# Output projections of all query blocks placed behind the attention loop, with three quarters of the next sum over the sequence

## The chip, the core and the metric

The kernel runs on one core of one Trainium2 chip. The metric is the device time of one execution in microseconds (us). A core has engines that run side by side, each with its own instruction queue: PE (TensorE, matrix products into PSUM), DVE (VectorE), ACT (ScalarE), POOL (GpSimd), and SP, which here does nothing but issue DMA transfers. PEld is the loading of PE's stationary operand. An instruction waits in its queue for the semaphores of what it needs, and what stands behind it in the same queue waits with it.

## What is computed

Four layers on x of 2048 positions by 512 features in bf16: a spectral layer (A), an attention layer (B), and both once more, each with a layer norm in front and a residual sum behind.

```python
def _A_ref(x, w_r, w_i):
    X = jnp.fft.rfft2(x.astype(jnp.float32), axes=(-2, -1)) * (w_r + 1j * w_i)
    return jnp.fft.irfft2(X, s=(S, D), axes=(-2, -1)).astype(jnp.bfloat16)

def _B_ref(x, wq, wk, wv, wo):          # 32 heads of 16, one key and value head
    q = (x @ wq).reshape(B, S, H, Dh).transpose(0, 2, 1, 3)
    k, v = x @ wk, x @ wv
    p = _softmax(jnp.einsum("bhqd,bkd->bhqk", q, k) * (Dh ** -0.5))
    o = jnp.einsum("bhqk,bkd->bhqd", p, v)
    return o.transpose(0, 2, 1, 3).reshape(B, S, H * Dh) @ wo

x = x + _A_ref(_layernorm(x), A_w_r, A_w_i)
x = x + _B_ref(_layernorm(x), B_wq, B_wk, B_wv, B_wo)
x = x + _A_ref(_layernorm(x), A_w_r, A_w_i)
x = x + _B_ref(_layernorm(x), B_wq, B_wk, B_wv, B_wo)
```

## The kernel before

x stays in SBUF as x_sb, 16 tiles of 128 positions by 512 features, named by r and t (position = 512 r + 4 p + t, p being the partition); xn_sb holds the normalised tiles in the same arrangement.

**Spectral layer.** The transform over the sequence is a matrix product by tables, split by t. over_s(t) takes, for each of four feature blocks b, four matmuls of xn_sb against the table FT (L218) and lets ACT copy the sum from PSUM into G (L220). DVE then combines the four t (over_t_even, over_t_odd: L228 to L239) into X, and over_d multiplies X by the feature table (L272). The way back ends in back_s, which writes x_sb and normalises it for the attention. Three calls of over_s come before over_t_even, the fourth behind it. The table FT has 2 MB and is loaded by four DMAs from SP (L202) into a buffer that the attention's transposed input xT used before it.

**Attention loop.** 32 groups g of four heads: group g belongs to query block g // 8 (512 positions). For each group and 16 blocks of keys there are 64 score tiles of 128 by 512. ACT takes three of every four (exponential of three tiles at once, L647), and DVE the fourth, by an integer trick in two instructions (L671, L677). So one group is 16 steps of the loop, and a layer 514. Each step issues its scores on PE (L569), the exponential, DVE's two instructions, and the product with the values of the step LAG = 2 before (pv_step, L659). That product and a row of denominators add up in one PSUM bank (pool psp, one buffer) over the group.

At the end of a group DVE copies that bank to o (evict, L584). The denominators are row 16 of each 32 and must be inverted and spread over the partitions: o to DRAM (d), back as 128 by 16 (den), a reciprocal on DVE (L592), to DRAM again, and four broadcast loads to rb (L597). POOL multiplies o by rb in three pieces (L614), each paced by DVE's work. Groups of even number write straight into ot (bf16, four column blocks for a query block); odd ones write od, and four DMAs (L617) move it 16 partitions on. At the end of a group the same PSUM bank also serves the query projection for group g + 2 (L437, copied by L442).

**Output projection.** When a query block is complete, outproj(k) multiplies a tile of 128 positions by wo in four matmuls (L627); DVE adds the residual (L631) and the layer norm follows: statistics on DVE (L142, L144), the rest on POOL (L148 to L153). In the last layer a DMA stores the tile instead (L774, by SP and POOL in turn). For the first three query blocks these 12 calls stand inside the loop, one in each of four groups (out_at), with the same PSUM bank; in such a step pv_step is put off. The last four calls stand behind the loop, after the denominators of group 31.

**Order.** chain() ties the instructions of PE, ACT, DVE and POOL inside the attention layer to the order in which the program issues them; SP's transfers are not tied. Elsewhere a scheduler orders them. The PSUM of the attention layer is six banks for two score buffers of three (psc), one for DVE's score tile (psd), one for psp.

Of the kernel before, what the change touches and what calls it, by code (L numbers as in the profile page):

```python
# [139 lines left out]
def layernorm_tile_pool(nc, lnpool, tabs, x_ap, xn_ap):  # L140
    stats = lnpool.tile([P, 6], F32, tag="ln_stats", bufs=4)
    nc.vector.bn_stats(stats, x_ap)  # L142
    mv = lnpool.tile([P, 2], F32, tag="ln_mv", bufs=4)
    nc.vector.bn_aggr(mv, stats)  # L144

    def rest():
        rstd = lnpool.tile([P, 1], F32, tag="ln_rstd", bufs=4)
        nc.gpsimd.tensor_scalar(out=rstd, in0=mv[:, 1:2], scalar1=EPS, scalar2=1.0, op0=ALU.add, op1=ALU.mult)  # L148
        nc.gpsimd.tensor_tensor(out=rstd, in0=rstd, in1=tabs["mhalf"], op=ALU.pow)
        nb = lnpool.tile([P, 1], F32, tag="ln_nb", bufs=4)  # L150
        nc.gpsimd.tensor_scalar(out=nb, in0=mv[:, 0:1], scalar1=rstd, scalar2=-1.0, op0=ALU.mult, op1=ALU.mult)
        for a in (0, 256):
            nc.gpsimd.tensor_scalar(out=xn_ap[:, a:a + 256], in0=x_ap[:, a:a + 256], scalar1=rstd, scalar2=nb,  # L153
                                    op0=ALU.mult, op1=ALU.add)
    return rest


R_OUTER = [(k // 4, k % 4) for k in range(16)]
# [32 lines left out]
def spectral_layer(nc, tc, tabs, shared, lnpool, x_sb, xn_sb, WT, WX, aw, loads):  # L191
# [5 lines left out]
    with (tc.tile_pool(name="workA", bufs=1) as work,  # L197
          tc.tile_pool(name="psA", bufs=6, space=bass.MemoryType.PSUM) as psum,
          tc.tile_pool(name="psB", bufs=2, space=bass.MemoryType.PSUM) as psum_b):
        FT = shared.tile([P, T, R, 512], BF, tag="big", bufs=1)  # L200
        for t in range(T):
            nc.sync.dma_start(out=FT[:, t], in_=tabs["src"]["FT"][:, t])  # L202
# [6 lines left out]
        G = work.tile([P, 4, T, 514], BF, tag="big", bufs=2)  # L209
        X = work.tile([P, 4, 2, 2, 4, 128], BF, tag="big", bufs=2)  # L210
        g.memset(G[:, :, :, 256:257], 0.0)


        def over_s(t):
            for b in range(4):
                ps = psum.tile([P, 512], F32, tag="pa")
                for r in range(R):
                    nc.tensor.matmul(ps, lhsT=xn_sb[:, r, t, b * P:(b + 1) * P], rhs=FT[:, t, r, :],  # L218
                                     start=(r == 0), stop=(r == R - 1))
                nc.scalar.copy(out=G[:, b, t, :].rearrange("p (s j) -> p s j", j=257)[:, :, 0:256],  # L220
                               in_=ps.rearrange("p (s j) -> p s j", j=256))
# [132 lines left out]
        U = work.tile([P, T, 2, 2, 512], BF, tag="big", bufs=2)  # L354
# [32 lines left out]
        for t in range(3):  # L387
            over_s(t)
# [35 lines left out]
def attention_inputs(nc, tabs, shared, xn_sb, aw):  # L424

    wq_sb, wka, wv_sb, vaug = aw["wq"], aw["wk"], aw["wv"], aw["vaug"]
    xT = shared.tile([P, NC, R * T, P], BF, tag="big", bufs=1)
# [3 lines left out]
    xTq = xT.rearrange("d c t p -> d c (t p)")  # L431
    QT = {}

    def qproj(g, ps):
        qb, hg = divmod(g, HG)
        for c in range(NC):
            nc.tensor.matmul(ps, lhsT=wq_sb[:, c, hg, :], rhs=xTq[:, c, qb * 512:(qb + 1) * 512],  # L437
                             start=(c == 0), stop=(c == NC - 1))
# [7 lines left out]
    def block(t, psum):  # L446
        for half in range(2):
# [4 lines left out]
            k = 4 * t + 2 * half  # L452
            dst = xT[:, :, k:k + 2, :].rearrange("d c i p -> d i c p")
# [6 lines left out]
        for c in range(NC):  # L460
            nc.tensor.matmul(ps, lhsT=wka[:, c, :], rhs=xTq[:, c, ks], start=(c == 0), stop=(c == NC - 1))
# [4 lines left out]
        for i in range(4):  # L466
            for c in range(NC):
                nc.tensor.matmul(psv[:, i, :], lhsT=xT[:, c, 4 * t + i, :], rhs=wv_sb[:, c, :],
# [25 lines left out]
def attention_layer(nc, tc, tabs, x_sb, xn_sb, aw, prep, epilogue_cb, in_order):  # L494
    with ExitStack() as ctx:
# [49 lines left out]
        for n0 in range(s0[NG]):  # L545
# [7 lines left out]
            if n in evict_at:  # L553
                n += 1
# [279 lines left out]
```

## Time and profile before

| what | us |
|---|---|
| median of three runs (1700.61 to 1702.69) | 1702.2 |
| the profiled execution | 1701.6 |
| its span, from first to last instruction | 1699.5 |
| ACT busy, DVE busy, PE busy in the span | 1496.0, 1554.9, 1410.2 |
| last exponential of the first attention layer ends | 836.14 |
| first matmul of over_d in the second spectral layer (L272) | 874.59 |
| last exponential of the second attention layer ends | 1675.72 |

Rows of the timeline are: start, duration, engine, line, operation, what it writes and reads, the number of instructions put together, and in brackets how long the engine had been idle before and what released it. So a single row with a long duration is a stretch in which the engine did not pause, and a bracket marks a pause.

### The profile page before, as it was taken

How to read it: one execution, taken by the hardware profiler on the slowest of the kernel's cores; microseconds unless marked ns; L12 is line 12 of the kernel's file. 1: busy time of each engine (PE TensorE's matmuls, PEld its weight loads, DVE VectorE, ACT ScalarE, POOL GpSimd, SP SyncE). 2: the span in 40 equal slices, each digit the busy share in tenths (PEclk: the TensorE clock that was granted, in tenths of full speed). 3: DMA queues.
4: the chain of work that ended last, by engine and by line, in shares of the span. 5: the costliest groups of instructions: out<-in, count | busy, mean ns of one | idle time of the engine just before them, and what ended most of it. 6: DMA issues, size and time to landing. Idle time of an engine off the chain costs nothing.

```text
span 1699.5 us, 32220 instructions
## 1 busy us (share of the span) xinstructions
PE 1410.2 (83%) x12732; PEld 460.5 (27%) x12732; DVE 1554.9 (91%) x2796; ACT 1496.0 (88%) x1225; POOL 204.8 (12%) x350
## 2 busy tenths in 40 slices
PE   6879888888888888888688888888888888888884
PEld 2432222222222222222133322222222222222221
DVE  6978999999999999999668689999999999999993
ACT  4369999999999999999633799999999999999994
POOL 3210000121001200210112100000110000001101
PEclk9988999999999999999888799999999999999997
DMA  7000000000000000001010000000000000000000
GB/s 269 1 1 8 16 17 16 16 13 14 16 16 16 16 16 17 15 16 60 23 51 1 1 8 17 16 17 19 23 20 16 20 23 15 17 17 22 20 17 28
DMA packets 47111, 40.24 MB, mean 24 GB/s; under 512 B 30832, under 2 KB 35184, under 8 KB 46704
## 3 DMA queue, kind: packets, MB, share of 16 engines
q1 hardware_dynamic: 46576, 37.14, 7.4%
q8 instruction: 99, 1.62, 0.4%
q0 software_dynamic: 384, 1.05, 0.2%
q14 instruction: 52, 0.43, 0.1%
HBM read 32.91 MB, written 3.15 MB: 21 GB/s over the span
## 4 chain that ended last, share of the span: by engine, by line
DVE 42%; ACT 21%; PE 19%; issue 15%; DMA 2%; POOL 1%; SPq 0%; DVEq 0%; POOLq 0%; ACTq 0%
ACT e L647 20%; DVE t_new L671 15%; DVE s_new L677 13%; PE pv_new L659 6%; PE dv L569 3%; DVE o L584 2%; PE sc L569 2%; DVE qt L442 2%; PE fd L272 2%; DVE qt L443 1%; PE ps L218 1%; DVE stats L125 1%; DVE x_sb L631 1%; PE ps L364 1%; PE ps L376 1%
## 5 line engine op out<-in xcount | busy, mean ns | idle before, releaser
L647 ACT ACTIVATE e<-sc 128x1536 bf16<-128x1536 f32 (+1 forms) x1028 | 1389.0, 1518 | 42.2 <-PE sc L569 41.6
L671 DVE TENSOR_SCALAR t_new<-dv 128x512 int16<-128x512 f32 x1016 | 691.2, 680 | 41.3 <-PE sc L569 23.2
L677 DVE TENSOR_SCALAR s_new<-t_new 128x2048 int16<-128x2048 int16 x1016 | 695.6, 686 | 0.0
L569 PE MATMUL dv<-qt,KT 32*128 32x512 bf16 x1016 | 388.2, 382 | 128.8 <-DVE t_new L671 118.6
L569 PE MATMUL sc<-qt,KT 32*128 32x512 bf16 x3080 | 420.9, 389 | 32.9 <-ACT e L647 3.2
L659 PE MATMUL pv_new<-s_new,vaug 128*32 128x512 bf16 x4064 | 413.2, 392 | 35.6 <-DVE x_sb L631 19.3
L659 PE MATMUL pv_new<-e,vaug 128*32 128x512 bf16 x3080 | 409.4, 385 | 0.4 <-ACT e L647 0.4
L569 PEld LDWEIGHTS <-KT 32*128 32x128 bf16 x4096 | 200.2, 91 | 718.9 <-issue 697.5
L659 PEld LDWEIGHTS <-vaug 128*32 128x32 bf16 x7144 | 138.3, 94 | 283.1 <-issue 264.7
L614 POOL TENSOR_TENSOR ot_new<-o,rb 128x176 bf16<-128x176 f32 (+1 forms) x96 | 56.0, 585 | 617.9 <-DVE s_new L677 480.5
L614 POOL TENSOR_TENSOR od<-o,rb 128x176 bf16<-128x176 f32 (+1 forms) x96 | 52.9, 554 | 517.3 <-DVE s_new L677 470.5
L437 PE MATMUL ps<-xT,wq_sb 128*128 128x512 bf16 x256 | 65.5, 378 | 10.7 <-DVE o L584 10.7
L627 PE MATMUL ps<-wo_sb,ot_new 128*128 128x512 bf16 x128 | 37.2, 416 | 40.0 <-DMA ot_new<-od 28.4
L272 PE MATMUL fd<-X,tab_DT 128*128 128x512 bf16 x256 | 56.1, 379 | 2.8 <-DVE X L239 2.8
L276 ACT CAST xn_sb<-fd 128x512 bf16<-128x512 f32 x32 | 18.8, 586 | 40.7 <-PE fd L272 40.7
L584 DVE COPY o<-pv_new 128x512 f32<-128x512 f32 x64 | 43.8, 684 | 8.5 <-issue 4.7
L364 PE MATMUL ps<-tab_PS,st 128*128 128x512 bf16 x128 | 35.4, 441 | 11.5 <-DVE st L312 10.2
L631 DVE TENSOR_TENSOR x_sb<-ps,x_sb 128x512 bf16<-128x512 f32 x32 | 21.7, 685 | 24.8 <-PE ps L627 24.8
L220 ACT CAST G<-ps 128x512 bf16<-128x512 f32 x32 | 17.9, 604 | 30.1 <-PE ps L218 30.1
L442 DVE CAST qt<-ps 128x512 bf16<-128x512 f32 x64 | 44.2, 690 | 0.1
L218 PE MATMUL ps<-FT,xn_sb 128*128 128x512 bf16 x128 | 32.2, 412 | 12.4 <-ACT xn_sb L134 11.1
L370 ACT CAST U<-ps 128x512 bf16<-128x512 f32 x24 | 14.1, 586 | 30.9 <-PE ps L364 30.9
(115 smaller groups left out, 603.6 us busy)
## 6 DMA issues: line engine op xcount, KB each, us to landing
rb<-d SPq DMA_DIRECT2D x256, 64.0 KB
FT<-const_FT SPq DMA_DIRECT2D x8, 512.0 KB
IT<-const_IT SPq DMA_DIRECT2D x8, 512.0 KB
x_sb<-in_A_x_dram SPq DMA_DIRECT2D x4, 512.0 KB
ot_new<-od SPq DMA_DIRECT2D x128, 16.0 KB
wr_raw<-in_A_w_r_dram SPq DMA_DIRECT2D x1, 1028.0 KB
wi_raw<-in_A_w_i_dram SPq DMA_DIRECT2D x1, 1028.0 KB
d<-o SPq DMA_DIRECT2D x64, 8.0 KB
```

Of the source, the lines that this page charges most:

```text
L218: nc.tensor.matmul(ps, lhsT=xn_sb[:, r, t, b * P:(b + 1) * P], rhs=FT[:, t, r, :], start=(r == 0), stop=(r == R - 1))
L272: nc.tensor.matmul(pss[i], lhsT=DT[:, b, w, 128 * fb:128 * fb + 128], rhs=X[:, b, part, c, :, :].rearrange("p k j -> p (k j)"), start=(b = ...
L364: nc.tensor.matmul(ps, lhsT=st[c][:, t, vec, q, fb, :], rhs=PS[:, fb, w, :], start=(k == 0), stop=(k == 3))
L437: nc.tensor.matmul(ps, lhsT=wq_sb[:, c, hg, :], rhs=xTq[:, c, qb * 512:(qb + 1) * 512], start=(c == 0), stop=(c == NC - 1))
L442: nc.vector.tensor_copy(out=qt, in_=ps)
L569: nc.tensor.matmul(dst, lhsT=KT[hs, kc * P:(kc + 1) * P], rhs=QT[g][hs, :], start=True, stop=True)
L584: nc.vector.tensor_copy(out=o, in_=pv.pop(g))
L614: pace(nc.gpsimd.tensor_tensor(out=dst[:, a:b], in0=o[:, a:b], in1=rb[:, a:b], op=ALU.mult))
L647: nc.scalar.activation(out=e[:, 0:na, :], in_=sc[:, 0:na, :], func=ACT.Exp, scale=SCALE)
L659: nc.tensor.matmul(pv[g][32 * h:32 * h + 32, :], lhsT=vaug[:, max(j, 0), kc, :], rhs=rhs, start=(first_pv[(g, h)] == u), stop=(last_pv[(g, ...
L671: nc.vector.tensor_scalar(out=tb[(g, kc // 4)][:, kc % 4, :], in0=dv, scalar1=T_MUL, scalar2=T_ADD, op0=ALU.mult, op1=ALU.add)
L677: image[0] = nc.vector.tensor_scalar(out=s_new, in0=tb[(g, b)], scalar1=0.5, scalar2=16384.0 + PH_OFF[j], op0=ALU.mult, op1=ALU.add)
```

## The change

The 12 calls of outproj inside the loop and their residuals and layer norms are gone from it, and with them out_at. All 16 calls are issued behind the loop, in triples of three tiles in one score buffer of three banks (triple), the first triple between the last two pv_steps, the second to fourth while the denominators of group 31 are under way, then the last query block without the odd half of its last column block. The residual is added by PE through an identity matmul in two of three tiles (one of three in the last layer) and copied by ACT, in the others by DVE (finish). The layer norm becomes four tiles at a time: statistics on DVE, a square root on ACT, the normalisation of one tile on ACT, one on POOL and two on DVE (normal). Three quarters of the next over_s (12 of 16 sums) follow in the same place, in score buffers (sequence); over_s(3) stays in the spectral layer, which from the second on calls no other.

The last group no longer moves od by DMA: two new tables, woE and woO, hold the even and odd half of wo's last column block, the other half zero, so od multiplies woO where it lies. They cost two memsets and eight small DMAs at the start. xT becomes four tiles in four buffers (big0 to big3). The FT tiles of the next layer come into them one at a time, two inside the loop, two behind it; the ot of query blocks 1 and 2 lie in big0 and big1. G and U move to a shared buffer. In the last layer all stores are issued by SP.

```diff
-        out_at = {s0[HG * (qb + 1) + 1 + i] + LAG + 1: 4 * qb + i for qb in range(NQB - 1) for i in range(4)}
...
-            if n in out_at:
-                n += 1
...
-        for n in range(s0[NG] + LAG + 1):
+        for n in range(s0[NG]):
...
-            elif n in out_at:
-                ps = psp.tile([P, 512], F32, tag="pv")
-                outproj(out_at[n], ps)
             else:
                 pv_step(n)
+            if nxt is not None and n in qproj_at and qproj_at[n] in (11, 15):
+                nxt["load"](qproj_at[n] // 4 - 2)
...
+            if g == NG - 1:
+                nc.gpsimd.tensor_tensor(out=dst, in0=o, in1=rb, op=ALU.mult)
+                otc["odd"] = dst
+                return
...
+        def outproj(k, ps, with_x, last_group=None):
...
+            terms = [(otc[qb][:, c, cols], wo_sb[:, c, :]) for c in range(4)]
+            if qb == NQB - 1:
+                terms[3] = (terms[3][0], aw["woE"])
+            if with_x:
+                terms.append((tabs["ident"], x_sb[:, r, t, :]))
+            if last_group:
+                terms = [(otc["odd"][:, cols], aw["woO"])]
...
+        def finish(k, ps, with_x):
+            t, r = divmod(k, 4)
+            if with_x:
+                nc.scalar.copy(out=x_sb[:, r, t, :], in_=ps)
+            else:
                 nc.vector.tensor_tensor(out=x_sb[:, r, t, :], in0=ps, in1=x_sb[:, r, t, :], op=ALU.add)
+            if store is not None:
+                store(r, t)
...
+        def triple(i):
+            ps = psc.tile([P, 3, 512], F32, tag="sc", name="tri")
+            for j in range(3):
+                outproj(3 * i + j, ps[:, j, :], j < n_x)
+            return ps
...
+        def normal(t):
...
+            nc.scalar.activation(out=rstd, in_=mv[t][:, :, 1], func=ACT.Sqrt, bias=tabs["eps"], scale=1.0)
+            nc.vector.reciprocal(rstd, rstd)
...
+            for r, eng in ((0, nc.scalar), (1, nc.gpsimd), (2, nc.vector), (3, nc.vector)):
...
+        def sequence(first):
...
+            ps = psc.tile([P, 3, 512], F32, tag="sc", name="seq")
+            for i, (t, b) in enumerate(units):
+                over_s_sums(nc, nxt, xn_sb, t, b, ps[:, i, :])
...
+        for n in range(s0[NG], s0[NG] + LAG):
+            pv_step(n)
+            if n == s0[NG]:
+                if nxt is not None:
+                    nxt["gather"]()
+                    dmys = lnpool.tile([P, 1], F32, tag="dmys", bufs=1)
+                p0 = triple(0)
+                triple_out(0, p0)
+            elif nxt is not None:
+                nc.scalar.activation(out=dmys, in_=tabs["eps"], func=ACT.Sqrt)
+        o, den = evict(NG - 1)
+        p1 = triple(1)
+        statistics((0, 1, 2))
+        triple_out(1, p1)
+        rb = invert(den)
+        p2 = triple(2)
+        statistics((3, 4, 5))
+        normal(0)
+        triple_out(2, p2)
+        normalise(NG - 1, o, rb)
+        if nxt is not None:
+            nxt["load"](2)
+        p3 = triple(3)
+        statistics((6, 7, 8))
+        normal(1)
+        triple_out(3, p3)
+        if nxt is not None:
+            nxt["load"](3)
...
+        pf = [ps_a[:, 0, :], ps_a[:, 1, :], ps_a[:, 2, :], ps_b]
         for i in range(4):
+            outproj(12 + i, pf[i], i % 2 == 0)
+        statistics((9, 10, 11))
+        normal(2)
+        q0 = sequence(0)
+        sequence_out(q0)
+        for i in range(4):
+            outproj(12 + i, pf[i], False, last_group=True)
+        for i in range(4):
+            finish(12 + i, pf[i], i % 2 == 0)
+        q1 = sequence(3)
+        statistics((12, 13, 14, 15))
+        sequence_out(q1)
+        normal(3)
+        for first in (6, 9):
+            q2 = sequence(first)
+            sequence_out(q2)
+        chain()
...
+    for name in ("woE", "woO"):
+        nc.gpsimd.memset(aw[name], 0.0)
...
+                nc.sync.dma_start(out=aw[("woE", "woO")[two]][32 * h:32 * h + 16, :], in_=wo_v[h, two][:, 3, :])
...
+    def store(r, t):
+        nc.sync.dma_start(out=out_v[:, r, t, :], in_=x_sb[:, r, t, :])
```

## The prediction

> **What bounds the kernel now.** I read ACT's own timeline first, since ACT runs almost without a pause in the loop, then who waited for the residual sums, then the chain of waits and the clock at the two ends.
>
> ACT in the first attention layer (start, us, the rows merged while ACT does not pause):
>
> ```profile
> 156.77 173.90 ACT L647 ACTIVATE e<-sc 128x1536 bf16<-128x1536 f32 x129 [0.45 <-PE sc L569]
> 331.94 21.66 ACT L647 ACTIVATE e<-sc 128x1536 bf16<-128x1536 f32 x16 [1.27 <-PE sc L569]
> 354.87 21.66 ACT L647 ACTIVATE e<-sc 128x1536 bf16<-128x1536 f32 x16 [1.27 <-PE sc L569]
> 377.81 21.66 ACT L647 ACTIVATE e<-sc 128x1536 bf16<-128x1536 f32 x16 [1.27 <-PE sc L569]
> 400.74 107.89 ACT L647 ACTIVATE e<-sc 128x1536 bf16<-128x1536 f32 x80 [1.27 <-PE sc L569]
> ...
> 756.64 79.50 ACT L647 ACTIVATE e<-sc 128x1536 bf16<-128x1536 f32 x59 [1.27 <-PE sc L569]
> ```
>
> The loop goes at ACT's pace (173.90 / 129 = 1.348 us a step). The first row runs through eight ends of groups, with their evictions and query projections, without a pause; the pauses stand once a group in the four groups that carry an output projection. They come from its residual sum: the value products wait until DVE has cleared the shared bank (the answer for L631, who waited for it; then one such row):
>
> ```profile
>   PE pv_new L659: 19.3, 24
> ...
> 329.90 0.59 PE L659 MATMUL pv_new<-s_new,vaug 128*32 128x512 bf16 x5 [0.80 <-DVE x_sb L631]
> ```
>
> 24 times is 12 in each layer. PE is strictly in order, so the next scores, and ACT, come late.
>
> The end of the first attention layer, as the chain of waits:
>
> ```profile
> 837.42 1.70 DMA d<-o
> 839.14 1.65 DMA den<-d
> ...
> 841.15 1.41 DMA d<-den
> ...
> 843.87 2.14 DMA rb<-d
> ...
> 846.17 1.56 POOL od L614 x3
> ...
> 857.38 14.13 PE ps L218 x56
> ```
>
> PE has nothing to do while 16 denominator rows go round, and wakes at half clock (start:end, length, busy us of PE, PEld, DVE, ACT, POOL, then granted clock, DMA share, GB/s):
>
> ```profile
> 836.00:838.00 2.00, 1.34 (x7) 0.36 (x6) 0.69 (x1) 0.14 (x1) 0.00 (x0) 1.00 0.00 0
> 838.00:840.00 2.00, 0.00 (x0) 0.00 (x0) 0.00 (x0) 0.00 (x0) 0.00 (x0) 1.00 0.01 4
> 840.00:842.00 2.00, 0.00 (x0) 0.00 (x0) 0.25 (x1) 0.00 (x0) 0.00 (x0) 0.68 0.04 4
> ```
>
> I count from T, the end of the last exponential: 756.64 + 79.50 = 836.14 in the first layer; over_d starts at 874.59 = T+38.45. In the second layer T = 1675.72, and the span's end is T+23.78.
>
> **Loop.** The pauses removed: 12 x 1.27 = 15.2 us; in the second layer ACT's timeline shows 12 of 1.17 to 1.18, 14.1 us. Together **-29.3**. A group then holds 16 x 2 x 0.60 (pitch of L671 and L677) + 0.69 (o) + 1.1 (qt) + 0.25 = 21.2 us of DVE against 21.57 of ACT: it still fits, as the 129 steps show. Bounds: nothing gained if evictions made the pauses (below); no more than 29.3, as ACT then never stops. SP's two FT loads in the loop (0.5 MB each) cost nothing: before, all four went there at 796 to 799 under the unbroken row of 756.64, though they delayed that group's rb to 806.45. POOL loses 0.19 + 0.55 + 0.26 + 1.10 us per tile and was idle anyway.
>
> **First layer, behind the loop.** Prices: a 512-column matmul at full clock 0.216 (four in 1.08 with the tail, L627), at half clock 0.43 (L218's rows at 858.19 and 858.62); an ACT copy 0.59, in a row 0.50 (eight L177 in 4.0); DVE residual 0.65 to 0.69; statistics of one tile 0.65 (pitch of L125 at 5.81, 6.46); square root 0.30; reciprocal and product of it 0.4; normalising on ACT 0.76, POOL 0.77; a pair on DVE has no such row: nearest is L488 (bf16, 512 columns, 404 ns), so 0.7, bounds 0.4 and 1.4. One rule comes from the built order of waits: if ACT and DVE both read one PSUM tile, the second waits for the first. The trace has this already:
>
> ```profile
> 960.28 0.22 ACT L473 ACTIVATE vaug<-psv 128x64 bf16<-128x64 f32 x1 [0.76 <-DVE vaug L475]
> ```
>
> So a triple is freed by its DVE residual behind ACT's copies and whatever stands ahead of both. Walk, in us after T. PE: triple 0 (14 matmuls) -0.95 to 2.1, last value products to 2.85, triple 1 to 5.9, triple 2 to 8.9, triple 3 to 11.9. Triple 0 is cleared at 4.0 and o copied by 4.75 (before: 1.25). Denominators: den 8.1; d<-den stands on SP behind FT(2), which waits for PE's tile 7 at 8.05, and its 0.5 MB goes first: 11.2 rather than 9.9; rb 15, product 16.6. DVE: statistics 0 to 2 until 6.65, residual 5 at 7.85, den, statistics 3 to 5 until 10.35, nb 10.8. ACT's normalising (11.55) holds copies 6, 7 until 12.6, residual 8 ends 13.35. Only then have tiles 12 to 15 a buffer: PE idles 1.45, works 13.35 to 17.25. The second round (statistics 15.3, nb 15.75, ACT 16.5, copies 17.55, residual 11 at 18.3) frees sequence 0: 18.3 to 20.9, woO to 21.8 (od has been ready for 4 us, so FT(2) costs nothing while that slack lasts). Third round: ACT normalises until 21.75, copies G until 23.35, tile 12, DVE 13, ACT 14 at 25.25: PE idles 21.8 to 25.3. Sequence 3 to 27.9, 6 to 30.5, 9 to 33.1. ACT: G to 29.6, root, normalising 31.05, G to 32.65, G to 34.8. over_s(3) needs those banks: 34.4 on, its second copy 36.9, then DVE 2.45 as before (872.16 to 874.59): over_d at T+39.3, **+0.9**. 12 projections, ten identity matmuls and their evictions fill the wait almost exactly. Lower bound: PE alone, 142 matmuls x 0.216 = 30.7 from T-0.95, 0.75 for the value products, and 3 us from the last sum to X: T+33.5, -4.9. Upper: +5 to +6, from the clock (below).
>
> The square-root table load (1.28 at 929.29) moves behind T+3.3, under PE's triples; at 929 it held the first root by about **-0.5** (0 to -1.28).
>
> **Second layer, behind the loop.** Residual 2 ends at 4.15, o 4.85. SP now carries 16 stores (0.36 each) in program order among the denominators: den<-d waits for store 4 (residual at 7.05) and goes at 7.5 rather than 6.6; d<-den behind store 6 at 9.6; rb behind store 9, whose copy needs triple 3 (11.95): 12.4 to 13.8, landed 16.0 against 1685.6 = T+9.9 before. Product 17.6, woO 18.55, evictions in turn 12 (19.2), 13 (19.9), 14 and 15 (20.6), and 3.15 to land the last store (2.8 from 1696.69 to 1699.5, and 0.35 for the store ahead): T+23.7, **-0.1**. What pays for the delay: no od transfer (1687.22 to 1691.0) and only one matmul a tile left. Bounds: -3.1 if rb waits for no store; +4 if the 13 stores' data, 128 KB each, go ahead at 400 GB/s. woE and woO: memsets on a POOL that is idle until 10.15, eight DMAs of about 0.42 behind wo's at 37; first read at 836. Hidden by 800 us.
>
> **Sum.** 1701.6 (profiled execution) - 29.3 + 0.9 - 0.5 - 0.1 = 1672.6; the median shown is 0.6 above that execution: **1673.2**.
>
> The clock: PE stopped at 837.3 and the clock fell at about 841.3 (0.68 in that window), 4 us later; in the second layer 3.5 (1676.9, 0.60 in 1680 to 1682). My pause at T+21.8 is 3.5 long: at the edge. If it falls, 24 matmuls cost 0.21 more: +5.1.
> The Trainium skill, page "TensorE: Matmul & The Clock Gate", section "Why this matters for your kernels", says to keep gaps between bursts under about 3 us or lose half the clock. By that rule the pause trips it, and the sum would be 1678; the two rows leave it open, and I go by the sum without it.
>
> **Rivals.** A, the hand-over stretches: the clock falls in the 3.5 us pause and in woO's wait (+5.1 and 4 x 0.21), 1679. For it: the pause; against: both drops came at the end of a longer one. B, engines overlap better than my walk: half of the way to both lower bounds, (5.8 + 3.0) / 2 = 4.4 less, 1669, or below. C, the change doesn't do what it says: the pauses belong to the eviction and the query projection and stay, 1702.5. Against: 129 steps without one. D, slower: with mostly waiting PE the clock stays at half through both ends, as it does for 956 to 984 (0.50). First layer 142 x 0.43 = 61.1, over_d at T+63.9: +24.6 on my walk; second, 70 x 0.43 = 30.1 and woO 1.7, end at T+36.8: +13.1; 1711. It makes the kernel slower only from 29.0 / 37.7 = 77% of those matmuls on; the clock is 1.00 at T and PE gets dense work, so it is unlikely.
>
> **Numbers.** Forecast 0.68, A 0.14, B 0.09, C 0.03, D 0.05; 0.01 left. The forecast's own range is 1669 to 1678; with A and B 1666 to 1682. About 0.2% (3.4 us) is what a measurement of this kernel tells from no change. Faster 0.92, same 0.03 (C), slower 0.05 (D).
>
> **What would show it.** ACT's loop rows without a 1.2 us pause; over_d near T+39 and PE's pauses near T+12, T+22; clock 1.00 between; rb of the last group near T+16. Wrong if pauses stay in the loop, if PE waits for od (woO) in the first layer, or if SP holds rb beyond T+18.

## The result, and the profile after

| | median us | range, runs | ratio to before, 95% interval |
|---|---|---|---|
| before | 1702.45 | 1700.61 to 1704.68, 4 | |
| changed | 1672.76 | 1669.72 to 1674.99, 4 | 0.9824 (0.9804 to 0.9844) |
| changed, again, on another chip | 1673.96 | 1673.39 to 1676.61, 5 | 0.9822 (0.9809 to 0.9835) |

The changed kernel is faster by 1.8%. Its profiled execution took 1673.17 us, with a span of 1671.4. The costliest group of instructions on the page of before and on that of the changed kernel (busy time, mean ns, idle time of ACT just before these instructions):

```profile
L647 ACT ACTIVATE e<-sc 128x1536 bf16<-128x1536 f32 (+1 forms) x1028 | 1389.0, 1518 | 42.2 <-PE sc L569 41.6
...
L669 ACT ACTIVATE e<-sc 128x1536 bf16<-128x1536 f32 (+1 forms) x1028 | 1386.4, 1526 | 16.0 <-PE sc L569 15.5
```

The exponentials are the same work as before (1389 and 1386 us of ACT); the idle time ahead of them was 42.2 us and is 16.0. ACT's timeline shows which part went, the first line from the first layer, the other two from the second:

```profile
161.14 662.83 ACT L669 ACTIVATE e<-sc 128x1536 bf16<-128x1536 f32 x492 [0.45 <-PE sc L569]
...
983.52 194.04 ACT L669 ACTIVATE e<-sc 128x1536 bf16<-128x1536 f32 x144 [0.49 <-PE sc L569]
...
1177.76 468.83 ACT L669 ACTIVATE e<-sc 128x1536 bf16<-128x1536 f32 x348 [0.20 <-PE sc L569]
```

Where twelve pauses of 1.27 us stood, 492 exponentials now follow each other without one (662.83 / 492 = 1.347 us a step). What is left of ACT's pauses stands at the start of each loop.

The first layer's end, PE's pauses, from its timeline (T = 823.97):

```profile
837.61 0.81 PE L647 MATMUL tri<-wo_sb,ot_new 128*128 128x512 bf16 x3 [1.66 <-DVE x_sb L655]
843.48 2.75 PE L192 MATMUL seq<-FT,xn_sb 128*128 128x512 bf16 x12 [1.82 <-DVE x_sb L655]
848.92 7.93 PE L192 MATMUL seq<-FT,xn_sb 128*128 128x512 bf16 x36 [1.83 <-ACT G L197]
858.51 3.61 PE L192 MATMUL ps<-FT,xn_sb 128*128 128x512 bf16 x16 [1.65 <-ACT G L197]
```

In place of one wait of 14.3 us (PE had nothing from 837.3 to 851.7) there are four short ones, none above 1.83 us. Where before the clock fell to a half after 4 us of nothing, it stays at full speed here (windows with the columns of the prediction's: the number behind POOL's busy time is the granted clock, the share of full speed at which TensorE was let run):

```profile
839.00:843.00 4.00, 2.66 (x13) 1.09 (x12) 3.15 (x8) 2.07 (x4) 2.17 (x2) 1.00 0.40 126
...
847.00:851.00 4.00, 2.17 (x11) 0.97 (x10) 1.96 (x5) 2.94 (x6) 0.82 (x1) 1.00 0.56 174
```

The second layer's end (T = 1646.59), SP's issues and what waits for them:

```profile
1653.86 0.38 SPq L588 DMA_DIRECT2D den<-d  x1
...
1657.87 0.25 DVE L592 RECIPROCAL den<-den 128x16 f32<-128x16 f32 x1 [3.86 <-DMA den<-d]
...
1658.15 0.33 SPq L594 DMA_DIRECT2D d<-den  x1
...
1660.18 1.79 SPq L597 DMA_DIRECT2D rb<-d  x4
...
1663.98 1.26 POOL L619 TENSOR_TENSOR od<-o,rb 128x512 bf16<-128x512 f32 x1 [21.24 <-DMA rb<-d]
```

Stage by stage (the two profiled executions; "kept" is the pair e12 and e11 below, the kernel before and the changed one with unread matmuls that keep the clock up; e11 also has a different second end):

| stretch, us | before | changed | difference | predicted | difference, kept |
|---|---|---|---|---|---|
| start to first exponential | 122.43 | 124.06 | +1.6 | 0 | +0.1 |
| first loop, to T | 713.71 | 699.91 | -13.8 | -15.2 | -16.9 |
| T to over_d | 38.45 | 39.51 | +1.1 | +0.9 | +0.6 |
| over_d to first exponential | 88.23 | 85.27 | -3.0 | -0.5 | -0.5 |
| second loop, to T | 712.91 | 697.84 | -15.1 | -14.1 | -15.6 |
| T to the span's end | 23.77 | 24.81 | +1.0 | -0.1 | |
| span | 1699.5 | 1671.4 | -28.1 | -29.0 | |

### The profile page after: what moved, and what is told of

The parts are those of the page before. It is cut to its first block, busy times and chain, and to the rows that moved or that the text cites. A ratio compares the mean times of both kernels' runs of the same rounds, so it can differ in the third digit from the quotient of the medians.

```text
span 1671.4 us, 32246 instructions
## 1 busy us (share of the span) xinstructions
PE 1421.6 (85%) x12756; PEld 459.7 (28%) x12756; DVE 1551.7 (93%) x2796; ACT 1505.6 (90%) x1250; POOL 158.4 (9%) x264
## 4 chain that ended last, share of the span: by engine, by line
DVE 39%; ACT 24%; PE 18%; issue 17%; DMA 1%; POOL 1%; SPq 0%; POOLq 0%; DVEq 0%; ACTq 0%
ACT e L669 23%; DVE t_new L693 15%; DVE s_new L699 12%; PE pv_new L681 6%; PE dv L569 3%; PE sc L569 2%; DVE o L584 2%; DVE qt L446 2%; PE fd L275 2%; DVE qt L447 2%; PE ps L192 1%; DVE stats L125 1%; PE ps L367 1%; PE ps L379 1%; DVE den L592 1%
## 5 line engine op out<-in xcount | busy, mean ns | idle before, releaser
L373 ACT CAST U<-ps 128x512 bf16<-128x512 f32 x24 | 14.1, 587 | 29.8 <-PE ps L367 29.8
L125 DVE BATCH_NORM_STATS2 stats<-x_sb 128x6 f32<-128x512 bf16 x48 | 31.8, 677 | 7.2 <-ACT x_sb L383 3.7
L441 PEld LDWEIGHTS <-wq_sb 128*128 128x128 bf16 x256 | 24.6, 96 | 39.7 <-issue 16.0
L275 PEld LDWEIGHTS <-tab_DT 128*128 128x128 bf16 x256 | 24.8, 98 | 32.8 <-issue 3.6
L379 PE MATMUL ps<-U,IT 128*128 128x512 bf16 x128 | 33.2, 379 | 0.0
```

The source lines that it names most:

```text
L275: nc.tensor.matmul(pss[i], lhsT=DT[:, b, w, 128 * fb:128 * fb + 128], rhs=X[:, b, part, c, :, :].rearrange("p k j -> p (k j)"), start=(b = ...
L379: nc.tensor.matmul(ps, lhsT=IT[:, t, part, c, r * P:(r + 1) * P], rhs=U[:, t, part, c, :], start=(k == 0), stop=(k == 3 and r % 2 == 1))
L441: nc.tensor.matmul(ps, lhsT=wq_sb[:, c, hg, :], rhs=xTq[qb][:, c, :], start=(c == 0), stop=(c == NC - 1))
```

## Experiments

All were timed beside the kernel before on the same chip; "end" and "loop" are the stretches of the table above, from each run's profile.

### e1 and e2: whose are the pauses?

e1 leaves the twelve calls out of the loop, e2 leaves their matmuls in and takes the reader away, the residual with the layer norm behind it (both edits to the kernel before; those rows of the result are missing):

```diff
-        out_at = {s0[HG * (qb + 1) + 1 + i] + LAG + 1: 4 * qb + i for qb in range(NQB - 1) for i in range(4)}
+        out_at = {}
```

```diff
-            later(1, residual)
+            if k >= 12:
+                later(1, residual)
```

> The kernel before, with the twelve output projections of each layer that stand in the loop over the keys left out (with their residuals, layer norms and stores, so those rows of the result are missing); the four of the last query block stay. My theory: each of the 24 pauses of the exponentials belongs to one of these calls. Measured between exponentials they cost 1.36 us each in the first layer (22.93 less sixteen exponentials of 1.348) and 1.28 in the second, so both loops together lose 16.3 + 15.4 = 31.7 us and the time falls from 1702 to 1670, or, by the idle times that the prediction added up, by 15.2 + 14.1 = 29.3 to 1673. Rival: the pauses belong to the eviction and the query projection that stand a step earlier in the same bank; then they stay and the time is 1702, less at most 24 x 0.3.

> The kernel before, in which the twelve output projections of each layer's loop keep their matmuls, but nobody reads what they wrote (their residuals on VectorE, layer norms and stores are left out, so those rows of the result are missing). Theory: most of a pause is the hand-over of the one bank (TensorE waits until VectorE's residual has read it, behind VectorE's own queue), so without a reader a pause shrinks from 1.3 us to 0.3 to 0.5, which is about the 4 x 0.216 us of added matmul time less what the score buffers ahead cover: 24 x 0.9 = 21 us less, 1681. Rival: a pause is the projection's own time on TensorE, which is full in the loop; then it stays above 1 us and the time is above 1695. Should it be as fast as the version without the projections (1670), TensorE had the room all along.

e1: 1673.14 us, ratio 0.9825 (0.9800 to 0.9849); loops 699.6 and 700.1 us. So a kernel that never does these calls is no faster than the changed one, which does them all. In the stretches they do cost something: e1's ends are 37.18 and 23.13 us, 2.3 and 1.7 shorter than the changed kernel's. In e1's profile 2.3 us more ahead of the second loop and 2.2 more in it hide that. The total happens to be the 1673 of the idle times, but the loops start slowly here too (below), so e1 does not tell the two prices of a pause apart. The rival is out.

e2: 1682.65 us, ratio 0.9878 (0.9857 to 0.9898). ACT's timeline of e2, from each of the two layers:

```profile
353.14 21.66 ACT L648 ACTIVATE e<-sc 128x1536 bf16<-128x1536 f32 x16 [0.30 <-PE sc L569]
...
1162.54 21.67 ACT L648 ACTIVATE e<-sc 128x1536 bf16<-128x1536 f32 x16 [0.30 <-PE sc L569]
```

With the same matmuls on PE and no reader, the pause falls from 1.27 and 1.17 to 0.30 us: about a quarter was PE's own time, the rest came with the reader. That it is the residual and not the layer norm behind it, e2 does not separate; the prediction's row for L659 (0.80 <-DVE x_sb L631) does. The loops, 702.8 and 706.6, lie 3.2 and 6.5 us above e1's. By the starts of the rows a pause costs 0.40 here, 12 x 0.40 = 4.8 a loop; the differences to that are of the size by which the loops' slow starts vary (below).

### The changed kernel again

> The changed kernel once more, beside the three that follow, with a second profile of it. If the 2 to 3 us by which the stretches ahead of the loops differ between the two first profiles come by chance (a dip of the granted clock at 80 to 84 us that only the changed kernel's profile has, and one at 912 to 924 that only the profile of before has), they stand elsewhere or are missing in this one, and the loops (699.9 and 697.8 us between the first exponential and the last matmul) and ends agree within 0.5 us. If they belong to the changed code, they are found at the same place.

The ratio came back (table on top). Stretches: 124.21, 700.46, 39.69, 87.10, 696.95, 24.09. The loops agree to 0.6 and 0.9 us rather than 0.5, and the stretch ahead of the second loop, 85.27 before, is 87.10 with the same code. So of its difference of -3.0 us to the kernel before, some 2 are chance. The dip of the clock at 80 to 84 us stands at the same place again (0.66 and 0.69 in these four us), which by the expectation would make it the changed code's; but e3, e4, e6 and e9 have the same code up to there and show 1.00. So it comes and goes.

### e3, e9, e10: the second layer's end

e3 holds the stores back behind the last four rb transfers, by an order among SP's issues. e9 also moves the first triple of the last layer behind evict, and e10 gives four of the stores to POOL's queue:

```diff
+        def release():
+            for r, t in held:
+                tc.add_manual_dep(store(r, t).ins, spread[0].ins.name, mybir.DependencyInfo(
+                    mybir.DependencyClass.NoSync, mybir.DependencyReason.DATA), reason="order")
+            held.clear()
...
         rb = invert(den)
+        release()
```

```diff
-                p0 = triple(0)
-                triple_out(0, p0)
+                    p0 = triple(0)
+                    triple_out(0, p0)
...
         o, den = evict(NG - 1)
+        if nxt is None:
+            p0 = triple(0)
+            triple_out(0, p0)
```

> The changed kernel with the stores of the last layer held back in the queue until the four transfers that spread the last denominators have been issued. In the profile of the changed kernel den<-d took 4.0 us from issue to landing in the second layer's end, with five stores of 128 KB issued ahead of it, and 1.65 in the kernel before; d<-den and rb follow it. Theory: the stores' data are what these small transfers wait for; the second layer's end falls from 24.8 us by 2.3 (den<-d back at 1.65) to 4 (the transfers behind it shorter too), the time from 1672.8 to about 1669.5. Rival: the transfers take that long by themselves behind the last matmuls; den<-d stays at 4.0, the end stays at 24.8 or grows by up to 1, with the stores that now come later: 1673 to 1674.

> The changed kernel with the last layer's stores held back, and in the last layer alone the first three output projections moved behind the last two steps of the loop, so that the copy that brings the last denominators out of PSUM stands ahead of them on TensorE and ahead of their residuals on VectorE. In the run with the stores held back the copy's transfer was issued at T+4.6 (T the end of the last exponential), the product ran at T+14.5 to 15.8, and the end took 22.8 us. The last step's matmuls wait for the last exponential, so the copy can stand at T+1.3 and its transfer at T+2.0. Theory: the chain of the denominators sets the end of this layer, and all of it moves ahead by 2.0 to 2.6: the end 20.4, the time 1669. Rival: the output projections and residuals on VectorE (16 in all, nine of 0.6 to 0.7 us each on VectorE) then last longer than the chain, since they start 3 us later; the end stays at 22 to 23.

> The kernel of the run before (the changed kernel, stores held back in the last layer, its first three projections behind the last steps of the loop), with four of the sixteen stores (the 10th, 12th, 14th and 16th) issued on GpSimd's queue, behind its last product. In the run before, the chain of the denominators did move ahead (the last rows were ready at T+19.2, in place of T+21.6 in the changed kernel's first profile), but the sixteen stores left SyncE in one row of 9.0 us, from 1653.7 to 1662.7, and the end came at 22.9 all the same. Theory: SyncE's issuing is what lasts longest there; with twelve stores it takes 6.8 us and ends before the last rows are ready, and the end falls to 20 to 21: 2 to 2.5 us less than the run before on equal stretches ahead. Rival: the stores' landing is what lasts; then the end stays at 22 to 23.

e3: 1672.59 us, ratio 0.9806 (0.9790 to 0.9822), which overlaps the changed kernel's beside it (0.9809 to 0.9835). The end is 22.84 us, against 24.81 and 24.09. SP's timeline of e3:

```profile
1655.28 0.34 SPq L588 DMA_DIRECT2D den<-d  x1
1657.35 0.34 SPq L594 DMA_DIRECT2D d<-den  x1
1659.88 1.71 SPq L597 DMA_DIRECT2D rb<-d  x4
```

From the issue of den<-d to that of d<-den it is 2.07 us, where it was 4.29 (1653.86 to 1658.15) in the first profile and 2.32 in the second. So that transfer was slow once with stores ahead of it, and not the next time; that the stores' data slowed it was not shown. What e3 took away both times is the stores' place in SP's queue ahead of den<-d, which goes at T+6.3 and not at T+7.3. rb is issued at T+10.9, against T+13.6 and T+12.2. The gain of the end, 1.3 to 2.0 us, is seen in the stretch and is below what the totals can show.

e9: 1671.33 us, 0.9827 (0.9806 to 0.9848), end 22.86: the rival's number. From SP's and DVE's timelines of e9, and the same reciprocal in e3:

```profile
1643.40 0.55 SPq L586 DMA_DIRECT2D d<-o  x1
...
1653.66 9.01 SPq L903 DMA_DIRECT2D out_dram<-x_sb  x16
```

```profile
1648.96 1.29 DVE L655 TENSOR_TENSOR x_sb<-tri,x_sb 128x512 bf16<-128x512 f32 x2 [1.52 <-ACT x_sb L653]
1650.16 0.24 DVE L592 RECIPROCAL den<-den 128x16 f32<-128x16 f32 x1
```

```profile
1657.07 0.25 DVE L592 RECIPROCAL den<-den 128x16 f32<-128x16 f32 x1 [0.70 <-DMA den<-d]
```

T is 1642.14 in e9 and 1648.95 in e3. The copy's transfer starts at T+1.3 as intended (T+4.6 in e3 and in the changed kernel), but the reciprocal, on DVE behind the residuals that now stand ahead of it, runs at T+8.0, against T+8.1 in e3: the move gained nothing for the chain. The last rows are ready at T+19.2, earlier than in the changed kernel (T+21.6) but not than in e3 (T+18.7), and the stores leave SP one by one until T+20.5, as in e3. So it is close to the rival's case: the residuals, moved later, hold the chain up. That the chain did move ahead, as e10's expectation says, was read against the changed kernel and not against e3.

e10: 1672.37 us, 0.9819 (0.9798 to 0.9840), end 23.18. SP's row of stores shrank to 6.24 us, and the last store left (from POOL) at T+20.0 in place of T+20.5, but the end did not move, so SP's issuing was not what lasted longest. Both theories failed here and the rivals' numbers came. From the last row to the end it took 4.0 us in e10, 4.1 in e3, 3.6 in e9 and 3.2 in the changed kernel; that the last stores land later when they come closer together would fit, and was not tested.

### e4: od by DMA again

```diff
-                otc["odd"] = dst
+                for h in range(4):
+                    nc.sync.dma_start(out=ot[32 * h + 16:32 * h + 32, hg // 2, :], in_=dst[32 * h:32 * h + 16, :])
...
+            odd = terms[3]
             if qb == NQB - 1:
-                terms[3] = (terms[3][0], aw["woE"])
+                terms = terms[:3]
...
-                terms = [(otc["odd"][:, cols], aw["woO"])]
+                terms = [odd]
```

> The changed kernel, in which the last group's product goes through four transfers to the other partitions again, as in the kernel before, in place of being multiplied by the weights that were laid out for it. In the kernel before such a move took 2.04 us (849.62 to 851.66). In the first layer the product ended at T+16.85 and its first matmul came at T+22.1, so 5.2 us were to spare: 0 there. In the second layer the matmuls wait for the product: 2.0 us more, less nothing, behind at most five stores up to 4. Sum: 2 to 4 us more than the changed kernel, 1675 to 1677. Rival: the move is covered in both layers by the residuals that queue on VectorE; then it stays at 1673. The shorter sum (four matmuls less per block of rows) is worth under 1 us.

1676.06 us, ratio 0.9830 (0.9817 to 0.9844). The second end is 28.88 us, 4.1 and 4.8 more than in the changed kernel's two profiles. The move's price, from e4's timeline:

```profile
1661.55 1.26 POOL L619 TENSOR_TENSOR od<-o,rb 128x512 bf16<-128x512 f32 x1 [20.88 <-DMA rb<-d]
...
1666.75 1.44 PE L649 MATMUL tri<-wo_sb,ot_new 128*128 128x512 bf16 x3 [8.13 <-DMA ot_new<-od]
```

From the product's end to the matmul it is 3.94 us, not the 2.04 I had taken, which was the last of the four alone. The four matmuls behind it then ran at a granted clock of 0.50 (1666 to 1668) and took 1.9 us, in place of 1.0 in the changed kernel. The first end is 40.29, 0.6 to 0.8 more: the transfer itself is covered, as expected, since the matmuls that read it did not wait (a stop of 2.77 us ahead of 839.47 took the clock to 0.50 there). The total shows only 2 to 3 us of the 4 to 5; in its one profile e4's first loop (696.75) is 3.2 and 3.7 us shorter than in the changed kernel's two, which would account for that.

### e5: the sums over the sequence behind the wait again

```diff
-        if loads:
-            for t in range(3):
-                over_s(t)
+        for t in range(3):
+            over_s(t)
...
-        q0 = sequence(0)
-        sequence_out(q0)
```

(and the three other sequences likewise).

> The changed kernel with all twelve sums over the sequence of the three first blocks back behind the last output projections, where the kernel before has them, in six PSUM buffers of one bank in place of two of three. Theory, from the walk through the first layer's end: the wait for the denominators is then shorter on TensorE, but ScalarE's and VectorE's work in it (copies, residuals, statistics) stays; TensorE has 12 x 4 matmuls of 0.216 = 10.4 us more to do after it, against the 5.8 us that it stood idle in that stretch of the changed kernel (pauses of 1.66, 1.82, 1.83 and some shorter). So the end grows by 0 to 5 us; I take 2: 1675. Rival: the pauses of the sums in three-bank buffers (1.83 and 1.65 us, for ScalarE's copies) cost as much as the overlap saves; then it is 1 to 2 us faster, 1671.

1677.45 us (1677.18 to 1677.64), ratio 0.9840 (0.9826 to 0.9853); the first end is 42.41 us, 2.9 and 2.7 more than in the changed kernel. That lies in the theory's range (0 to 5, 2 taken), but more than half of its cause was not in the theory. PE's timeline, and the clock in the windows around that pause, of e5:

```profile
849.20 15.62 PE L192 MATMUL ps<-FT,xn_sb 128*128 128x512 bf16 x64 [6.61 <-ACT x_sb L652]
```

```profile
845.00:846.00 1.00, 0.00 (x0) 0.00 (x0) 0.66 (x2) 0.27 (x1) 0.00 (x0) 0.87 0.75 258
846.00:847.00 1.00, 0.00 (x0) 0.00 (x0) 0.87 (x4) 0.56 (x2) 0.40 (x1) 0.50 1.03 389
...
852.00:853.00 1.00, 1.00 (x5) 0.35 (x4) 0.57 (x4) 0.53 (x2) 0.00 (x0) 0.72 0.00 0
```

Without the sums PE stands still from 842.6 to 849.2. Taking the windows with 0.87 and 0.72 as those in which the clock goes from 1.00 to 0.50 and back, it falls 3.2 us after PE stopped and comes back 3.4 us after it began again. 36 such matmuls take 7.93 us at full clock in the changed kernel, so 64 would take 7.93 + 28 x 0.216 = 14.0; here they take 15.62. So some 1.6 of the 2.8 us are the clock: read so, the sums in the wait are worth more by keeping PE awake than by their own overlap. This is rival A's mechanism after a long stop. No run kept the clock up in e5, so the share is worked out from these rows and not tested.

### e6, e8, e11, e12: the clock at the loops' starts

The dips of the clock ahead of and in the loops' starts differ from profile to profile, which blurs every difference of 2 or 3 us. These four put matmuls that nobody reads where PE waits: e6 ahead of the loops, e8 also between the halves of the inverse transform (with e3's order), e11 also ahead of the loop's first five steps (with e10's end), e12 the same ones in the kernel before.

```diff
+            for _ in range(n):
+                nc.tensor.matmul(idle[0], lhsT=tabs["ident"], rhs=aw["wo"][:, 0, :], start=True, stop=True)
...
+            if n < 5:
+                sc_n = psc.tile([P, 3, 512], F32, tag="sc", name="sc")
+                first[n] = sc_n
+                for i in range(2):
+                    nc.tensor.matmul(sc_n[:, i, :], lhsT=tabs["ident"], rhs=wo_sb[:, 0, :], start=True, stop=True)
```

> The changed kernel with 34 matmuls more per layer whose result nobody reads (the identity by the output weights, 0.216 us each at full clock), put where TensorE waits in the last two blocks of projections ahead of the loop and while the keys are scaled (4, 6, 7, 4 and 13 of them). In the changed kernel's profile the granted clock is 0.50 to 0.64 from 116 to some 145 us and from 942 to 967 us, from the stretches on in which TensorE is busy for 1.5 to 2.2 of 4 us, and the loop then runs its first 25 us slowly. Theory: the clock falls because TensorE has too little to do there. Kept busy it stays at 1.00; the pauses of the exponentials at the two loops' starts (6.3 and 4.6 us in the changed kernel's profile) shrink to some 2 each, and the last blocks of projections are 1 to 2 us shorter: 8 to 11 us less, about 1664. Rival: the clock falls with the loop's own first matmuls (32 rows, or the wait for its first exponential), whatever stands ahead; then the added matmuls cost 0 to 7 us and the time is 1673 to 1680.

> The kernel of the run before this one, with the last layer's stores held back behind the last denominators' spread as well (the end of the second layer fell from 24.8 and 24.1 to 22.8 us by that), and with 13 further unread matmuls in the first layer and 28 in the second between the two halves of the inverse transform over the channels, where TensorE stood still for 2.9 us in the first layer and 2.0 + 3.4 in the second, and where the dips of the clock at 80 to 84 and 912 to 924 us came and went between profiles. Theory: it takes those dips away as well (1 to 3 us each where they come) and with them most of the spread between executions: 1660 to 1662, spread under 2 us. Rival: the dips have another cause; then the time is that of the run before less 1.5, and the spread of 3 to 5 us stays.

> The kernel of the run beside it, with all the unread matmuls of the wider version (ahead of the loops), and two more of them ahead of each of the loop's first five steps, written into the score buffers before the scores. With the unread matmuls ahead of the loops the clock stayed at 1.00 up to them but fell to 0.50 at 125 and 948 us, some 3 us into the loops, where TensorE was busy 0.6 of each us, and came back 15 to 25 us later. Theory: it falls by the first steps' low activity; kept busy through them it stays at 1.00, both loops lose their slow starts, 3 to 5 us each: loops of 693 to 696 us in place of 698 to 699, the time 1658 to 1662. Rival: it falls with the loop itself, whose matmuls use 32 of the rows or of the columns, whatever stands between them; then the loops stay at 697 to 700 and the time is that of the wider version less the end's 2: 1666.

> The kernel before with the same unread matmuls (ahead of the loops, and two ahead of each of the loop's first five steps). In the changed kernel they held the clock at 1.00 and gave loops of 693.9 and 692.6 us and a time of 1656.6 with a spread of 2.5. This run prices the removed pauses without the slow starts, which were 2 to 3 us longer or shorter from one profile to the next. Theory: a pause is worth its whole 1.36 and 1.28 us, so the loops are 16.3 and 15.4 us longer than those: 710.2 and 708.0; with this kernel's own ends (38.5 and 23.8) and starts as in the changed kernel kept busy (122.4 and 85.0) the span is 1687.9 and the time 1689.7. By the prediction's idle times (15.2 and 14.1) the loops are 709.1 and 706.7 and the time 1687.3. Rival: part of the change's gain was the clock, which fell less in the changed kernel; then the loops differ by under 13 us each and the time is below 1684.

e6: 1669.61 us, ratio 0.9808 (0.9789 to 0.9827), too close to the changed kernel's to call. Windows of e6 at the first loop's start (its first exponential begins at 121.35):

```profile
122.00:124.00 2.00, 1.37 (x11) 0.29 (x7) 1.26 (x2) 2.00 (x2) 0.00 (x0) 1.00 0.00 0
124.00:126.00 2.00, 1.83 (x11) 0.35 (x10) 0.81 (x2) 2.00 (x3) 0.00 (x0) 0.58 0.00 0
```

The clock, which fell at some 119 us in the changed kernel, now lasts into the loop, and falls there, at some 124. The slow stretch was put off, not removed: in this the rival was right, while the time lies between the theory's 1664 and the rival's 1673.

e8: 1668.99 us, 0.9804 (0.9782 to 0.9825). The clock is 1.00 in its profile at 76 to 88 and at 904 to 924 us, and the stretch ahead of the second loop is the shortest of all (84.81); the loops still start slowly (698.0 and 699.3), and the spread stayed at 5.5 us (1665.78 to 1671.32): close to the rival's numbers, not the theory's 1660 to 1662.

e11: 1656.56 us (1655.49 to 1658.04), ratio 0.9730 (0.9710 to 0.9750), against 0.9819 (0.9798 to 0.9840) of e10 beside it: the theory's case. The same place in e11:

```profile
120.00:124.00 4.00, 3.51 (x19) 1.08 (x17) 2.83 (x8) 1.85 (x3) 0.00 (x0) 1.00 0.00 0
124.00:128.00 4.00, 4.00 (x27) 0.85 (x25) 1.77 (x3) 4.00 (x4) 0.00 (x0) 1.00 0.00 0
```

The loops take 693.94 and 692.62 us. Ten matmuls more per layer, 2.2 us of PE, on top of those ahead of the loop, keep its start at full speed up to 148 us, where a dip of some 3 us follows (0.57 in 148 to 152). It is the fastest version of this study.

e12: 1688.47 us (1685.89 to 1690.31), ratio 0.9916 (0.9902 to 0.9929). Its loops, 710.87 and 708.23, are 16.9 and 15.6 us longer than e11's. Its timeline still shows the pauses whole:

```profile
351.90 21.66 ACT L664 ACTIVATE e<-sc 128x1536 bf16<-128x1536 f32 x16 [1.27 <-PE sc L586]
374.84 21.66 ACT L664 ACTIVATE e<-sc 128x1536 bf16<-128x1536 f32 x16 [1.27 <-PE sc L586]
```

374.84 - 351.90 = 22.94 for sixteen steps of 1.348, so 1.37 us a pause, and 16.4 for twelve; the half microsecond above that goes with a dip at 150 to 154 us, which is deeper in e12 (0.50) than in e11 (0.79). In the second layer 15.6 stands against 12 x 1.28 = 15.4. These are one profile each, and e12's is of its slowest execution. The medians differ by 31.9 us, and the four stretches outside the loops add up to 269.4 and 269.2, so some 31.8 belong to the loops: the price by starts (31.8), not the one by idle times (29.3).

## Why the prediction was right

Predicted 1673.2 us, measured 1672.8 and 1674.0.

**The pauses belong to the residual's hand-over of the bank: shown** by e1 (without the calls the loop is as short as the changed one) and e2 (without the reader the pause is 0.30), with the trace's row that names the residual. Rival C is out. Rival B, better overlap at both ends, did not come: both ends are longer than predicted, not shorter.

**The size of the loop's term, -29.3: the total agrees (-28.9), by luck, for two errors that cancel.** The step that failed is "12 x 1.27" with its bound "no more than 29.3, as ACT then never stops". The bracket of a pause counts ACT's idle time, but consecutive exponentials overlap by some 0.1 us (1.45 us each at a pitch of 1.348), and a pause also costs that overlap. By the starts of the rows it is 1.37 and 1.28 us, 31.8 together, and with the clock kept up e12 and e11 differ by 32.5. Against that stood a term that the sum put at nothing: the loops' slow starts, 713.71 - 710.87 = 2.8 and 4.7 us in the profile of before, 6.0 and 5.2 in that of the changed kernel. Over the nine profiles that have the changed kernel's loops as they are (its own two, e3 to e6 and e8 to e10), a loop is between 2.8 and 6.5 us longer than e11's in the first layer and 4.3 to 7.6 in the second. The values of before lie in both ranges, at their lower ends, so chance is enough to explain the difference; that it is chance was not shown beyond that.

**The first layer's end, +0.9: +1.1, +1.2, and +0.6 with the clock kept up.** The walk held in most of its steps: o copied at T+4.7 (4.75 in the walk), the reciprocal at T+8.1 (8.1), d<-den issued behind FT(2) at T+8.4 and rb, which waits for it, at T+12.1 (11.2 for d<-den's landing), the product at T+16.9 (16.6), over_d at T+39.5 (39.3). PE's pauses are 1.66 us before T+13.6 (1.45 before 13.35) and 1.82 before T+19.5 (1.05 before 18.3). The statistics of one tile were put too low: from one tile's start to the next it is 0.80 us on DVE behind the loop (828.58, 829.40, 830.20), not 0.65. The third pause was too large: 1.83 us, not 3.5, since PE was later by then.

**Rival A, the clock in that pause: did not come** in the changed kernel's two profiles, where the pause was 1.8 us long and not 3.5. That it was short is not the whole reason. In e3, whose first layer has the same code, the pause before it was 1.96 us long and the clock fell, 3.1 us after the last matmul, when PE was already back at work (PE's row, and the window around it):

```profile
842.28 4.18 PE L192 MATMUL seq<-FT,xn_sb 128*128 128x512 bf16 x12 [1.96 <-DVE x_sb L655]
```

```profile
842.00:846.00 4.00, 3.72 (x12) 1.50 (x12) 3.46 (x11) 0.89 (x2) 0.46 (x1) 0.68 0.00 0
```

Twelve matmuls took 4.18 us there and 2.75 in the changed kernel; the end grew by only 0.4 to 0.6 us (40.08), as the next pause shrank to 0.54. So A's mechanism is real, its price of 5.1 us was too high for this place, and that the first two profiles missed it was partly luck. The length of a stop alone does not decide: 1.93 us left the clock at 1.00 (the second profile of the changed kernel), as did 2.96 in that profile's second end, while 1.96 took it in e3 and at 912 us in the kernel before. The rule that the prediction quoted (the Trainium skill, "TensorE: Matmul & The Clock Gate", "Why this matters for your kernels": gaps under about 3 us) fits the 6.6 us of e5, but does not hold for the stops of 1.96 us. What else decides was not tested.

**The table load, -0.5:** -0.5 with the clock kept up (85.54 to 85.01); no run moved the load alone. The -3.0 between the two first profiles goes with a dip of the clock at 912 to 924 us that of these two only the profile of before had, and the +1.6 at the start with the dip at 80 to 84 that only the changed kernel's had: with the clock kept up the start differs by 0.1.

**The second layer's end, -0.1: +1.0 and +0.3.** Mis-sized were the denominators' transfers behind the stores: den<-d was issued at T+7.3, as said (7.5), but landed 4.0 us later in the first profile, and the reciprocal, at T+11.3, held two residuals behind it on DVE; d<-den then went at T+11.6, not 9.6, and the product ended at T+18.7, not 17.6. In the second profile d<-den went at T+9.6, as said, and the end was 0.3 longer. With the stores out of their way (e3) the end is 22.8. The removed od transfer took 3.9 us in e4, where the prediction's row had 3.8; with the half clock behind it the end is 4.1 to 4.8 longer there.

**Rival D (half clock through both ends): did not come;** in both profiles of the changed kernel the clock is 1.00 through the first end, and in the second up to the last matmul. Slow matmuls behind a wait cost some 1.6 us in e5.

## What to carry to other kernels

Price a pause by the starts of the rows on both sides, not by the idle time in the bracket: pipelined instructions overlap, and each pause also costs one overlap. Work whose result another engine must read can cost a loop more than its own time if it shares the loop's only bank: take it to a wait that is there anyway, and fill that wait densely, since by e5's rows more than half of what the sums in the wait brought here was the clock. When a move is meant to pull a chain ahead, follow the chain to its next step on every engine: in e9 the copy came 3.3 us earlier and the reciprocal 0.1. And before differences of 2 to 3 us are explained, keep TensorE busy in both kernels and compare them again; here that brought the loops, the first end and the stretch behind it to within 0.6 us of what the starts of the rows and the prediction's walk give.

## What the runs showed that I had not expected

The clock does not need a long stop to fall. At the loop's start PE is busy 0.6 of each microsecond, in matmuls that use 32 of the rows, with gaps of at most 0.56 us (e8, from 122.0 on), and the clock falls to 0.50 at 125.4:

```profile
123.00:124.00 1.00, 0.59 (x4) 0.10 (x4) 0.54 (x2) 1.00 (x1) 0.00 (x0) 1.00 0.00 0
...
125.00:126.00 1.00, 0.76 (x7) 0.22 (x4) 0.45 (x1) 1.00 (x2) 0.00 (x0) 0.72 0.00 0
```

It then stays there for 17 us in e8, and from 118.8 to 153 in the changed kernel's first layer, although PE is busy nearly all the time from the loop's fourth step on, where after a stop with dense matmuls behind it (e5) it was back after 3.4 us. Two matmuls of full height ahead of each of the first five steps kept it up through the start (e11). Why it comes back so late in the loop was not tried; whether the clock goes by the rows in use or by the time in use is open.

An unchanged loop was 2.8 to 7.6 us longer than e11's, and changed by up to 3.7 us from one profile to the next. Whether the spread between executions goes with it is not clear: it was 5.3 and 3.2 us in the changed kernel's two series, 2.5 in e11's and 4.4 in e12's, of four to six runs each.
